# Spreading a softmax over the steps of a matmul loop, and moving its sums to another PSUM bank

## The chip, the cores and the metric

One core of a Trainium2 chip. The metric is device time in microseconds, the median of several executions. All runs quoted were fast, at a granted TensorE clock of 0.995 to 1.000. Single executions of one kernel mostly lie within 1 us of each other; now and then one is 1 to 2.7 us longer.

## The reference, cut to what matters

```python
qn = q / (np.linalg.norm(q, axis=1, keepdims=True) + 1e-06)     # B, N, C = 4, 5824, 256
kn = k / (np.linalg.norm(k, axis=1, keepdims=True) + 1e-06)
s = kn.transpose(0, 2, 1) @ qn / tau                            # 256 x 256 per batch
a = softmax(s)                                                  # over the last axis
x = (v @ a).reshape(B * N, C)
out = ((x @ w1) * (x @ w2)) @ w3 @ w_out                        # 1024 wide inside
```

The softmax is small (256 x 256 per batch). Nearly all the work is the chain of matmuls over 23,296 tokens.

## The kernel before

For each batch the kernel folds the softmax matrix into w1 and w2 ("folds", eight products into `Wf`). Then it runs 11 chunks of 512 tokens and one short chunk of 192 columns. A chunk has eight **steps**. A step makes two products a and b (two matmuls of 512 columns each), evacuates a with ScalarE (`as`), multiplies it with b on VectorE (`abs`), and multiplies an earlier `abs` by the last weights into `out`, two steps behind.

During batch b the kernel also prepares batch b+1: the products G of q and k, their norms, the softmax, the folds. These are items of an agenda. Each has a time on the kernel's own schedule clock, which advances by the estimated TensorE time of what is emitted, and items come out between two steps only.

```python
def k_row():                      # norms of k, four ScalarE operations in a row
    ...
    nc.scalar.activation(out=kr, in_=src, func=AF.Ln)
    nc.scalar.activation(out=kr, in_=kr, func=AF.Exp, scale=0.5)
    nc.scalar.activation(out=kr, in_=kr, func=AF.Ln, bias=eps_t)
    nc.scalar.activation(out=kr, in_=kr, func=AF.Exp, scale=-1.0)
...
def scale(ct):                    # VectorE reads G
    nc.vector.tensor_mul(st["s"][:, ct, :], G_tiles[n][:, ct, :], st["kr"])

def exps():                       # ScalarE
    for ct in range(CT):          # CT = 2
        nc.scalar.activation(out=e[:, ct, :], in_=st["s"][:, ct, :], func=AF.Exp, scale=st["r"][:, ct : ct + 1])

def scaled():
    for ct in range(CT):
        scale(ct)
    exps()
...
# PSUM tiles of 512 fp32: G 1, ab 4 (a, b, folds, sums), out 3
st["sum"] = psum.tile([P, 512], F32, tag="out" if n == 0 else "ab", ...)
...
head = [(0.0, norms), (0.0, k_row), (0.0, q_sums)]      # q_sums ends with r: two small ScalarE operations
return head + [(0.0, scaled), (0.2, sums)] + [(0.43, lambda i=i: fold(i)) for i in range(8)]
...
def run_due(upto=None):           # called between steps
    lim = clock[0] if upto is None else upto
    while agenda and agenda[0][0] <= lim:
        ...
...
ts = [t1 + 1.0] + [t1 + late + t for t in (8.5, 9.0, 11.0, 14.5)] + [t1 + late + 15.5 + 0.9 * i for i in range(8)]
```

## Time and profile before

| | before |
|---|---|
| median | 575.26 us (6 runs, 574.97 to 577.88; the prediction had the first three, 575.4) |
| span of the profiled run | 573.5 us |
| TensorE busy | 559.5 us, 98% |
| idle TensorE around the softmax of batches 1, 2, 3 | 0.60, 1.07, 1.07 us |

A busy share is how much of the span an engine had work in it. TensorE at 98% still leaves 14 us idle: 7.2 in the first 40 us, 4.0 in the last 13.5, and 2.7 around the three softmaxes. I also use one measure that the profile doesn't print: the **stretch** from the first full-width product a of one batch to that of the next, from the starts in the timeline of TensorE, in the one profiled execution of each kernel. Each contains one softmax, it includes idle time that modelled matmul ends hide, and it doesn't see the start of the kernel.

| stretch with the softmax of batch | before |
|---|---|
| 1 (40.53 to 182.70) | 142.17 us |
| 2 (to 316.47) | 133.77 us |
| 3 (to 449.91) | 133.44 us |
| the rest, to the last matmul (569.41) | 119.50 us |

The last has no softmax; it is 119.49 or 119.50 in all twelve profiled kernels, so this measure can tell tenths of a microsecond apart. The lines of the profile before are shown in the prediction.

### The profile page before, as it was taken

What the parts mean: (1) busy time and instruction counts of PE and PEld (TensorE: products, weight loads), DVE (VectorE), ACT (ScalarE), POOL (GpSimd) and SP (SyncE); (2) the same over time, 40 slices, a digit from 0 to 9 for tenths busy, and PEclk for the clock granted to TensorE, in tenths of its full rate; (3) what the DMA queues carried; (4) which work ended last, traced back from release to release, by engine and by line L of the source; (5) the groups of instructions that cost most, each with busy time, mean ns of one, the idle gap of its engine ahead of it and who ended that gap; (6) DMA issues with size and microseconds to landing.
All of it is one profiled execution on the core that took longest, in us unless ns stands there. A gap on an engine that the chain in (4) does not pass through costs nothing.

```text
span 573.5 us, 10096 instructions
## 1 busy us (share of the span) xinstructions
PE 559.5 (98%) x3744; PEld 354.8 (62%) x3750; DVE 377.3 (66%) x612; ACT 337.4 (59%) x624; POOL 82.9 (14%) x164
## 2 busy tenths in 40 slices
PE   8889999999999999999999999999999999999997
PEld 4755576776665666666666666666665666666565
DVE  1047744788877567887776567778876656565564
ACT  0046635777856567776756567767756554454453
POOL 5250020312030111111030012021120000000000
PEclk9999999999999999999999999999999999999999
DMA  8999959769675698495661595675740325221011
GB/s 161 211 194 209 179 99 240 183 153 234 137 174 118 137 191 151 91 192 120 145 147 55 113 203 132 133 142 120 183 110 38 84 73 147 63 62 75 38 70 59
DMA packets 74560, 76.93 MB, mean 134 GB/s; under 512 B 54160, under 2 KB 58256, under 8 KB 74512
## 3 DMA queue, kind: packets, MB, share of 16 engines
q0 software_dynamic: 15504, 39.46, 38.9%
q1 hardware_dynamic: 58784, 36.64, 22.1%
q8 instruction: 29, 0.48, 0.3%
q10 hardware_dynamic: 224, 0.20, 0.1%
q14 instruction: 19, 0.16, 0.1%
HBM read 78.91 MB, written 23.86 MB: 179 GB/s over the span
## 4 chain that ended last, share of the span: by engine, by line
PE 86%; DMA 6%; ACT 4%; DVE 2%; issue 1%; POOL 1%; ACTq 0%; DVEq 0%; POOLq 0%
PE o L470 26%; PE a L429 26%; PE b L429 26%; PE G L188 5%; DMA k<-in_k_dram 5%; PE fold L348 2%; ACT as L435 2%; DVE abs L444 1%; DMA w<-in_moe_w_dram 1%; PE w L587 1%; ACT e L311 0%; POOL k L109 0%; ACT kr L273 0%; POOL q L109 0%; DVE osb L491 0%
## 5 line engine op out<-in xcount | busy, mean ns | idle before, releaser
L444 DVE TENSOR_TENSOR abs<-as,b 128x512 bf16<-128x512 bf16 x336 | 229.9, 686 | 141.0 <-ACT as L435 130.4
L435 ACT CAST as<-a 128x512 bf16<-128x512 f32 (+1 forms) x384 | 215.3, 562 | 179.4 <-DVE abs L444 92.2
L429 PEld LDWEIGHTS <-Wf 128*128 128x128 bf16 x1536 | 149.2, 98 | 102.6 <-issue 2.1
L429 PE MATMUL a<-vT,Wf 128*128 128x512 bf16 x704 | 209.4, 379 | 0.5 <-ACT as L435 0.5
L470 PE MATMUL o<-W_sb,abs 128*128 128x256 bf16 x1376 | 209.6, 273 | 0.1
L429 PE MATMUL b<-vT,Wf 128*128 128x512 bf16 x704 | 209.3, 379 | 0.0
L470 PEld LDWEIGHTS <-abs 128*128 128x128 bf16 x1376 | 134.4, 98 | 81.6 <-DVE abs L446 0.3
L197 DVE TENSOR_TENSOR acc<-acc,sq 128x1024 f32<-128x1024 f32 x66 | 80.4, 1219 | 0.2 <-ACT sq L185 0.2
L188 PE MATMUL G<-k,q 128*128 128x256 bf16 x276 | 49.7, 273 | 0.0
L185 ACT ACTIVATE sq<-q 128x512 f32<-128x512 bf16 x66 | 41.8, 633 | 0.0
L185 ACT ACTIVATE sq<-k 128x512 f32<-128x512 bf16 x66 | 41.6, 630 | 0.0
L417 POOL COPY gate_t<-abs 1x1 bf16<-1x1 bf16 x39 | 13.8, 354 | 168.8 <-DVE abs L444 167.9
L491 DVE COPY osb<-o 128x512 f32<-128x512 f32 x44 | 30.1, 685 | 0.7 <-PE o L470 0.7
L188 PEld LDWEIGHTS <-q 128*128 128x128 bf16 x276 | 27.0, 98 | 3.1
L421 POOL COPY gate_t<-vT 1x1 bf16<-1x1 bf16 x17 | 4.3, 255 | 170.3 <-DMA vT<-v 161.8
L490 ACT COPY osb<-o 128x512 f32<-128x512 f32 x44 | 25.8, 586 | 4.1 <-PE o L470 2.1
L271 ACT ACTIVATE kr<-row 128x256 f32<-128x256 f32 x1 | 0.4, 383 | 31.6 <-PE row L266 31.6
L109 POOL DMA_DIRECT2D q<-in_q_dram x29 | 15.6, 539 | 12.9 <-DMA k<-in_k_dram 5.6
L348 PE MATMUL fold<-w,e 128*128 128x512 bf16 x61 | 16.8, 379 | 0.5 <-DMA w<-in_moe_w_dram 0.2
L355 ACT ACTIVATE Wf<-fold,rs 128x512 bf16<-128x512 f32 x16 | 10.9, 687 | 7.9 <-PE fold L348 6.5
L109 POOL DMA_DIRECT2D k<-in_k_dram x25 | 13.7, 548 | 3.9 <-DMA k<-in_k_dram 1.9
L109 POOL DMA_DIRECT2D v<-in_v_dram x25 | 13.5, 543 | 4.0 <-issue 2.7
(90 smaller groups left out, 227.2 us busy)
## 6 DMA issues: line engine op xcount, KB each, us to landing
out_dram<-osb SPq DMA_DIRECT2D x44, 512.0 KB, 3.0
k<-in_k_dram POOLq DMA_DIRECT2D x19, 512.0 KB, 8.6
v<-in_v_dram POOLq DMA_DIRECT2D x19, 512.0 KB, 5.3
q<-in_q_dram POOLq DMA_DIRECT2D x18, 512.0 KB, 6.5
w_wout<-in_moe_w_dram POOLq DMA_DIRECT2D x1, 2048.0 KB, 23.4
k<-in_k_dram POOLq DMA_DIRECT2D x4, 320.0 KB, 9.8
v<-in_v_dram POOLq DMA_DIRECT2D x4, 320.0 KB, 5.5
q<-in_q_dram POOLq DMA_DIRECT2D x4, 256.0 KB, 11.9
```

What stands on the lines that cost most here:

```text
L109: nc.gpsimd.dma_start(out=pieces[nm, n, pi][:, lo:hi, :], in_=qk_main[nm, n][0][:, pi * PIECE + lo : pi * PIECE + hi, :])
L185: nc.scalar.activation(out=dst[:, :, part, :], in_=src[:, o : o + 2, :], func=AF.Square)
L188: nc.tensor.matmul(G[:, ct, :], lhsT=qt[:, i, ct * P : (ct + 1) * P], rhs=kt[:, i, :], start=(pr == 0 and part == 0 and ct == 0), stop=(pr ...
L197: nc.vector.tensor_add(accs[n], accs[n], sqs[0])
L348: nc.tensor.matmul(st["fold", i], lhsT=st["e"][:, c2, c1 * P : (c1 + 1) * P], rhs=w12[:, c2, w, h * 512 : (h + 1) * 512], start=(c2 == 0), ...
L417: nc.gpsimd.tensor_copy(gate_t, last_ab[0][:1, :1])
L429: nc.tensor.matmul(t[:, :n], lhsT=Wf[b][:, ct, w, j * P : (j + 1) * P], rhs=rhs_of(b, c, ct), start=(ct == 0), stop=(ct == CT - 1),)
L435: nc.scalar.copy(a_sb[:, :n], tiles[0][:, :n])
L444: nc.vector.tensor_mul(ab, a_sb, tiles[1])
L470: nc.tensor.matmul(tl[h][:, o, :], lhsT=lhsT, rhs=W_sb[:, j, :], start=(j == 0 and o == 0), stop=(j == FT - 1 and (small or o == 1)), skip ...
L490: nc.scalar.copy(o[:, 0:2, :], tl[0])
L491: nc.vector.tensor_copy(o[:, 2:4, :], tl[1])
```

## The change

Its intent: the softmax of batches 1 to 3 no longer comes as bursts on ScalarE but as single operations between evacuations, and its sums no longer take one of the four ab buffers but the bank of G, which is idle once the scales have read it.

```diff
-            kr = work.tile([P, C], F32, tag="kr", name=f"kr_{n}", bufs=1)
-            nc.scalar.activation(out=kr, in_=src, func=AF.Ln)
-            ... (three more)
+            st["row"] = src
+            st["kr"] = work.tile([P, C], F32, tag="kr", name=f"kr_{n}", bufs=1)
+            if n == 0:
+                for i in range(4):
+                    k_step(i)
+
+        def k_step(i):
+            kr = st["kr"]
+            nc.scalar.activation(
+                out=kr, in_=kr if i else st["row"], func=(AF.Ln, AF.Exp)[i % 2],
+                scale=(1.0, 0.5, 1.0, -1.0)[i], bias=eps_t if i == 2 else 0.0,
+            )
 ...
-                st["sum"] = psum.tile([P, 512], F32, tag="out" if n == 0 else "ab", name=f"sum_{n}", bufs=3 if n == 0 else 4)
+                st["sum"] = psum.tile([P, 512], F32, tag="out" if n == 0 else "G", name=f"sum_{n}", bufs=3 if n == 0 else 1)
 ...
-        head = [(0.0, norms), (0.0, k_row), (0.0, q_sums)]
-        return head + [(0.0, scaled), (0.2, sums)] + [(0.43, lambda i=i: fold(i)) for i in range(8)]
+        return (
+            [(0.0, 0.0, norms), (0.0, 6.0, k_row)]
+            + [(0.0, 6.0 + 1.3 * i, lambda i=i: k_step(i)) for i in range(4)]
+            + [(0.0, 6.5, q_sums), (0.0, 9.3, lambda: q_norm(st["ss"]))]
+            + [(0.0, 11.3 + 1.3 * ct, lambda ct=ct: scale(ct)) for ct in range(CT)]
+            + [(0.0, 12.0 + 1.3 * ct, lambda ct=ct: exps(ct)) for ct in range(CT)]
+            + [(0.2, 15.5, sums)]
+            + [(0.43, 16.5 + 0.85 * i, lambda i=i: fold(i)) for i in range(8)]
+        )
 ...
-            t0, t1 = 57.0, 116.0
+            t0, t1 = 57.0, 115.5
 ...
-        late = 2.5 if b == 0 else 0.0
-        ts = [t1 + 1.0] + [t1 + late + t for t in (8.5, 9.0, 11.0, 14.5)] + ...
+        for i, (cst, t, fn) in enumerate(soft):
+            at(t1 + 1.0 + t + (2.0 if b == 0 and i > 0 else 0.0), cst, fn)
```

(`exps` takes the half as an argument, and batch 0 calls the same operations in the old order. By its new times the change also moves the scales, the sums and the folds up to two clock units later.)

More of the change, by code (lines that the diff above doesn't have):

```diff
@@ L250, in scaled_first @@
             scale(1)
-            exps()
+            exps(0)
+            exps(1)
         def norms():
@@ L269, in k_row @@
                 src = st["tot"][:, 1, :]
-            kr = work.tile([P, C], F32, tag="kr", name=f"kr_{n}", bufs=1)
-            nc.scalar.activation(out=kr, in_=src, func=AF.Ln)
-            nc.scalar.activation(out=kr, in_=kr, func=AF.Exp, scale=0.5)
-            nc.scalar.activation(out=kr, in_=kr, func=AF.Ln, bias=eps_t)
-            nc.scalar.activation(out=kr, in_=kr, func=AF.Exp, scale=-1.0)
-            st["kr"] = kr
+            st["row"] = src
[9 more added lines that the diff above has]
+            )
         def diagonal(src):
@@ L290, in q_sums @@
         def q_sums():
-            q_norm(diagonal(st["tot"][:, 0, :].rearrange("p (c t) -> p c t", t=P)))
+            st["ss"] = diagonal(st["tot"][:, 0, :].rearrange("p (c t) -> p c t", t=P))
         def q_norm(src):
@@ L306, in scale, with exps @@
             nc.vector.tensor_mul(st["s"][:, ct, :], G_tiles[n][:, ct, :], st["kr"])
-        def exps():
-            e = work.tile([P, CT, C], BF16, tag="e", name=f"e_{n}", bufs=2)
-            for ct in range(CT):
-                nc.scalar.activation(
-                    out=e[:, ct, :], in_=st["s"][:, ct, :], func=AF.Exp, scale=st["r"][:, ct : ct + 1]
-                )
-            st["e"] = e
-        def scaled():
-            for ct in range(CT):
-                scale(ct)
-            exps()
+        def exps(ct):
+            if ct == 0:
+                st["e"] = work.tile([P, CT, C], BF16, tag="e", name=f"e_{n}", bufs=2)
+            nc.scalar.activation(
+                out=st["e"][:, ct, :], in_=st["s"][:, ct, :], func=AF.Exp, scale=st["r"][:, ct : ct + 1]
+            )
         def sum_mm(c2):
             if c2 == 0:
-                st["sum"] = psum.tile([P, 512], F32, tag="out" if n == 0 else "ab", name=f"sum_{n}", bufs=3 if n == 0 else 4)
+                st["sum"] = psum.tile([P, 512], F32, tag="out" if n == 0 else "G", name=f"sum_{n}", bufs=3 if n == 0 else 1)
                 Wf[n] = wf_pool.tile([P, CT, 2, F], BF16, tag="Wf", name=f"Wf_{n}")
@@ L377, in soft_units @@
             return [k_first, k_row, q_first, scaled_first, first_folds] + [lambda i=i: fold(i) for i in range(6, 8)]
-        head = [(0.0, norms), (0.0, k_row), (0.0, q_sums)]
-        return head + [(0.0, scaled), (0.2, sums)] + [(0.43, lambda i=i: fold(i)) for i in range(8)]
+        return (
[6 more added lines that the diff above has]
+            + [(0.43, 16.5 + 0.85 * i, lambda i=i: fold(i)) for i in range(8)]
+        )
     clock = [0.0]
@@ L648, in make_agenda @@
         soft = soft_units(n)
-        late = 2.5 if b == 0 else 0.0
-        ts = [t1 + 1.0] + [t1 + late + t for t in (8.5, 9.0, 11.0, 14.5)] + [t1 + late + 15.5 + 0.9 * i for i in range(8)]
-        for t, (cst, fn) in zip(ts, soft):
-            at(t, cst, fn)
+        for i, (cst, t, fn) in enumerate(soft):
+            at(t1 + 1.0 + t + (2.0 if b == 0 and i > 0 else 0.0), cst, fn)
         agenda.sort()
```

## The prediction

> **What bounds the kernel now.** I read the page first, then the waits of TensorE, then busy time by stretch, then the timeline around a softmax.
>
> ```profile
> PE 559.5 (98%) x3744; PEld 354.8 (62%) x3750; DVE 377.3 (66%) x612; ACT 337.4 (59%) x624; POOL 82.9 (14%) x164
> ...
> PE 86%; DMA 6%; ACT 4%; DVE 2%; issue 1%; POOL 1%; ACTq 0%; DVEq 0%; POOLq 0%
> ```
>
> TensorE is the bound: busy 98%, and 86% of the chain that ended last. Busy could hide slowness, so I checked the pace. One step of the main loop is four matmuls of 512 columns (a and b) and four of 256 (out), and it starts every 1.30 us (a at 419.68, 420.98, 422.28), which is full rate at a granted clock of 0.999. So only idle time of TensorE can be won, and where it idles is told by its waits.
>
> ```profile
> PE sqq L221 <- DMA q<-in_q_dram: 3.9, 3, 2.1
> PE sum L327 <- ACT as L435: 1.6, 2, 0.8
> PE sum L327 <- ACT e L311: 1.2, 1, 1.2
> ...
> PE a L429 <- ACT as L435: 0.7, 3, 0.2
> ```
>
> The DMA wait and the 1.2 us for e belong to batch 0 at the start, which the change leaves alone. What remains is the softmax of batches 1 to 3. By stretch (length, busy PE, PEld, DVE, ACT, POOL, clock, DMA):
>
> ```profile
> 172.00:184.00 12.00, 11.40 (x82) 6.87 (x81) 8.38 (x28) 7.94 (x18) 0.66 (x2) 1.00 0.60 132
> 184.00:292.00 108.00, 108.00 (x696) 67.85 (x694) 81.28 (x110) 73.56 (x132) 18.11 (x36) 1.00 0.69 147
> ...
> 300.00:304.00 4.00, 2.93 (x22) 1.67 (x20) 2.66 (x7) 2.42 (x5) 0.00 (x0) 1.00 0.61 185
> ...
> 434.00:438.00 4.00, 2.93 (x22) 1.67 (x20) 2.66 (x7) 2.42 (x5) 0.00 (x0) 1.00 0.35 135
> ```
>
> TensorE idles 0.60, 1.07 and 1.07 us in the three softmaxes and nowhere in the 108 us between two of them. **The most that a perfect softmax saves is about 2.7 us**, 0.5%, plus small gaps that matmul ends hide. The timeline of batch 3 shows the cause:
>
> ```profile
> 431.33 0.42 ACT L274 ACTIVATE kr<-kr 128x256 f32<-128x256 f32 x1
> 431.66 0.19 ACT L295 ACTIVATE r<-ss 128x2 f32<-128x2 f32 x1
> 431.88 0.20 ACT L296 ACTIVATE r<-r 128x2 f32<-128x2 f32 x1
> 431.99 1.05 ACT L435 CAST as<-a 128x512 bf16<-128x512 f32 x2
> ...
> 434.39 0.75 DVE L306 TENSOR_TENSOR s<-G,kr 128x256 f32<-128x256 f32 x2
> ...
> 434.84 0.91 ACT L311 ACTIVATE e<-s,r 128x256 bf16<-128x256 f32 x2 [1.31 <-DVE s L306]
> ...
> 435.65 1.05 ACT L435 CAST as<-a 128x512 bf16<-128x512 f32 x2
> ...
> 436.26 0.24 PE L327 MATMUL sum<-ones_b,e 128*128 128x1 bf16 x4 [0.82 <-ACT as L435]
> ...
> 436.75 0.59 PE L429 MATMUL a<-vT,Wf 128*128 128x512 bf16 x2 [0.25 <-ACT as L435]
> ```
>
> Undisturbed, evacuations (as) start every 1.30 us: 428.11, 429.41, then due at 430.71, 432.01, 433.31, 434.61. The first burst of six small ScalarE operations makes one start at 431.99, 1.28 us late, and TensorE does not stop. The second burst, two exps behind a wait for s, makes one start at 435.65, 2.34 us late, and TensorE stops for 0.82 us: the sums need a buffer of the ab group, and all four are full. **So about 1.3 us of lateness is absorbed.** By arithmetic: an evacuation starts 0.63 us after its product and takes 0.58, and its buffer is wanted 2.60 after the product, so 1.39 is the slack.
>
> **What the Trainium skill says.** "TensorE: Matmul & The Clock Gate", "Wait — 56ns, not 53.3ns?": start to start is N/2.4 GHz plus about 2.5 ns; 4x215.8+4x109.2 = 1300 ns, and the trace agrees (1.30). The same page, "Architectural detail: the array is 16× 32×32, not 1× 128×128": ScalarE and VectorE are strict FIFO. The trace agrees: the evacuation due at 433.31 stands behind the exps, though its product began at 432.68. "ScalarE: Activation LUTs", "What ACT_TABLE_LOAD costs": an ACTIVATE takes 186 ns + 0.833 per element, 93 more for each pointer operand, and neighbours overlap by about 93. For 256 elements: 399, and 492 with the pointer; the trace has 417, 508 (bias) and 500 (exp), with as to as 0.47 apart. "PSUM — Partial Sum Buffer", "Specifications (TRN2)": eight banks of 2 KiB. The kernel has G 1, ab 4, out 3: none is free for the sums but G's own, idle once s is read.
>
> **The change, part by part.** It removes and adds no instruction; batch 0 runs as before.
>
> (1) The four kr operations and the two of r are spread. That burst cost nothing, so this wins nothing itself.
>
> (2) The sums go to G's bank. They no longer wait for an evacuation, only for e, and the ring of four is not lent out for a product.
>
> (3) scale and exp are split per half. The aim is a scale in one step and its exp in the next. Whether that happens is set by the kernel's own schedule clock: a step charges 1.300 and items come out only between steps. I worked the boundaries out. In batch 1 (softmax of 2) they are at 12.065+1.3m (two first steps 1.945, scores 46x0.22), in batch 2 (softmax of 3) at 12.283+1.3m, in batch 0 (softmax of 1) at 18.567+1.3K. For batch 2 the scales at 116.3 and 117.6 come out at m=81 and 82, and the exps at 117.0 and 118.3 also at 81 and 82. The same for batch 3. **So each exp still stands directly behind its scale**, only one pair per step. For batch 1 they do separate: scales at K=86, 87, exps at 87, 88.
>
> Cost of a pair in one step, from starts in the trace: evacuation to product on VectorE 0.62 (160.92 to 161.54), to s 0.60 (433.79 to 434.39), to exp 0.45 (434.39 to 434.84), exp to next evacuation 0.40 (half of 434.84 to 435.65): 2.07 instead of 1.30, 0.77 late. Two in a row: 1.54 late, for batch 2 some 0.15 more, because its fourth kr operation comes in one step with an output copy. Against 1.39: TensorE stops 0.15 to 0.3, partly while it runs the sums. Batch 3 has another snag: its first fold comes out in the same step as the sums, and its evacuation waits on ScalarE for the reciprocal, about a step; I put 0.3 there, and 0.1 for four folds in a row in batch 2.
>
> Sum: batch 2, 1.07-0.15-0.1 = 0.8; batch 3, 1.07-0.15-0.3 = 0.6; batch 1: the first product of its short chunk starts at 173.67 instead of the due 173.29, and its outputs at 174.40 instead of 173.62, so 0.78 if all goes. There the folds also come a step or two later, into short steps that lose about 0.8 us between them (17,920 columns take 7.6 us at the pace above, the stretch 173.67 to 182.70 took 9.03; part of that is the stop): fewer steps share with a fold, perhaps 0.1. Together 2.3. All of it is on the path, since TensorE is the path from 62 us on. 575.4-2.3 = **573.1, put at 573.2**.
>
> **Rivals.** (A) The exps behind their scales stop TensorE as much as before, only at another place: for it, the coinciding steps in batches 2 and 3 and the VectorE queue, where s stands behind a 0.69 us product; against it, the halves are a step apart and 1.3 us was absorbed before. Then only batch 1 gains: 574.5 to 575. (B) All stalls vanish, the short chunk included: 575.4-2.7-0.6 = 572.1. (C) An earlier kr waits for the all-reduce on GpSimd (3.23 us): for batch 1 it ends at 165.73 and the first kr would stand behind the output copy at about 165.9; for batch 3 it ends at 427.44 and kr is due at 427.3. A wait of 0.2 inside the slack: nothing. (D) More buffers for the ring start transfers earlier: no, loads are gated by products.
>
> **Range and chances.** B gives the lower end, A the upper, and runs of the same kernel lie from 575.35 to 577.88, most within 0.1. 8 in 10: 572.2 to 575.2. A gain of 2% would need 11.5 us, four times all the idle time there is; a loss of 2% would need a new stall of 4 us in each softmax. Chances: faster 0.01, same 0.98, slower 0.01.
>
> **What would show it.** Right: TensorE's waits no longer list the sums behind an evacuation; kr operations stand singly between evacuations; in batches 2 and 3 each exp still shows a wait for s of some 0.6 to 1.2 us; idle in those softmaxes falls from 1.07 to below 0.5. Wrong: idle stays near 1 us there (A), the folds' evacuations show waits of over 1 us for rs, or the sums wait for e by more than 0.3. It would be far off only if the rotation of the ab buffers brought a stall into every step, which nothing in the diff does.

## The result, and the profile after

The kernel after takes **573.24 us** (median of 6, 572.82 to 573.53) against 575.26. The ratio of the two is 0.9959, 95% interval 0.9942 to 0.9976. A ratio here is the mean time of one kernel's fast runs over that of the other's of the same rounds, so not quite the ratio of the medians. The prediction said 573.2, range 572.2 to 575.2.

The page after, busy line and chain that ended last:

```profile
PE 559.4 (98%) x3750; PEld 354.5 (62%) x3750; DVE 377.4 (66%) x612; ACT 337.7 (59%) x624; POOL 83.3 (15%) x164
...
PE 92%; DMA 5%; DVE 1%; ACT 1%; POOL 1%; issue 0%; ACTq 0%; POOLq 0%
```

The work is the same, to 0.1 us of TensorE. ScalarE's part of the chain fell from 4% to 1%: the end is less often set by an evacuation. TensorE's waits after (total, times, longest):

```profile
PE sqq L221 <- DMA q<-in_q_dram: 3.9, 3, 1.9
PE sum L328 <- ACT e L318: 1.2, 1, 1.2
...
PE a L438 <- ACT as L444: 0.3, 1, 0.3
```

The 1.6 us of sums behind evacuations are gone, and of 0.7 us of products behind evacuations 0.3 is left. By stretch (length, busy PE, PEld, DVE, ACT, POOL, clock, DMA):

```profile
172.00:184.00 12.00, 11.86 (x87) 7.21 (x86) 8.85 (x27) 7.81 (x19) 0.53 (x1) 1.00 0.61 132
...
300.00:304.00 4.00, 3.89 (x28) 2.41 (x27) 1.91 (x5) 2.35 (x5) 0.00 (x0) 1.00 0.46 153
...
434.00:438.00 4.00, 4.00 (x28) 2.26 (x27) 2.51 (x6) 1.85 (x4) 0.00 (x0) 1.00 0.15 54
438.00:450.00 12.00, 11.59 (x83) 7.28 (x81) 8.44 (x25) 7.60 (x17) 0.00 (x0) 1.00 0.11 45
```

Idle TensorE is now 0.14, 0.11 and 0.00 us where it was 0.60, 1.07 and 1.07. But the last row idles 0.41 us, where the kernel before has this:

```profile
438.00:450.00 12.00, 11.95 (x88) 8.11 (x88) 8.97 (x23) 7.29 (x17) 0.00 (x0) 1.00 0.11 42
```

So in batch 3 something is given back later. The stretches say how much:

| stretch with the softmax of batch | before | after | gain |
|---|---|---|---|
| 1 | 142.17 | 141.43 | 0.74 |
| 2 | 133.77 | 132.76 | 1.01 |
| 3 | 133.44 | 133.21 | 0.23 |

Their sum is 1.98; the profiled run after entered batch 0's first product 0.16 later (40.69), which leaves 1.83, and the profiled spans differ by just that (573.5 to 571.7). What ScalarE does around the softmax of batch 3 after the change, from its timeline:

```profile
430.42 0.59 ACT L444 CAST as<-a 128x512 bf16<-128x512 f32 x1
431.07 0.59 ACT L499 COPY osb<-o 128x512 f32<-128x512 f32 x1
431.72 0.59 ACT L444 CAST as<-a 128x512 bf16<-128x512 f32 x1
433.40 0.51 ACT L318 ACTIVATE e<-s,r 128x256 bf16<-128x256 f32 x1 [1.09 <-DVE s L313]
433.81 0.57 ACT L444 CAST as<-a 128x512 bf16<-128x512 f32 x1
435.47 0.51 ACT L318 ACTIVATE e<-s,r 128x256 bf16<-128x256 f32 x1 [1.09 <-DVE s L313]
435.88 1.06 ACT L444 CAST as<-a 128x512 bf16<-128x512 f32 x2
438.13 0.69 ACT L356 ACTIVATE Wf<-fold,rs 128x512 bf16<-128x512 f32 x1 [1.19 <-DVE rs L335]
```

Each exp waits 1.09 us for its scale (bracketed: how long the engine stood idle before, and for whom): the two are in one step, not apart, as the prediction had worked out. From one evacuation to the next it is 2.09 and 2.07 us (predicted 2.07), so the second is 1.56 late (predicted 1.54). Then the first fold's evacuation holds ScalarE 1.19 us for the reciprocal of the sums. TensorE pays behind that:

```profile
438.29 1.65 PE L349 MATMUL fold<-w,e 128*128 128x512 bf16 x6
440.07 0.59 PE L438 MATMUL a<-vT,Wf 128*128 128x512 bf16 x2
...
441.37 1.46 PE L349 MATMUL fold<-w,e 128*128 128x512 bf16 x6
442.66 0.33 PE L438 MATMUL a<-vTt,Wf 128*128 128x192 bf16 x2
...
446.60 0.33 PE L438 MATMUL a<-vTt,Wf 128*128 128x192 bf16 x2 [0.27 <-ACT as L444]
```

Three folds take 1.78 us to the next product (438.29 to 440.07), the next three 1.29: 0.49 lost, and 0.27 more in the short chunk.

### The profile page after: what moved, and what is told of

Same layout as the page of the kernel before. It is cut to its first block, busy times and chain, and to the rows that moved or that the text cites. A ratio compares the mean times of both kernels' runs of the same rounds, so it can differ in the third digit from the quotient of the medians.

```text
span 571.7 us, 10102 instructions
## 1 busy us (share of the span) xinstructions
PE 559.4 (98%) x3750; PEld 354.5 (62%) x3750; DVE 377.4 (66%) x612; ACT 337.7 (59%) x624; POOL 83.3 (15%) x164
## 4 chain that ended last, share of the span: by engine, by line
PE 92%; DMA 5%; DVE 1%; ACT 1%; POOL 1%; issue 0%; ACTq 0%; POOLq 0%
PE o L479 28%; PE a L438 27%; PE b L438 27%; PE G L188 5%; DMA k<-in_k_dram 5%; PE fold L349 2%; PE w L596 1%; ACT as L444 0%; ACT kr L279 0%; POOL k L109 0%; POOL q L109 0%; DVE abs L453 0%; PE sqk L221 0%; DVE vT L136 0%; DVE abs L455 0%
```

## The experiments

**Theory.** What counts is how late an evacuation starts against its due time, which is 0.63 us after the start of its product. Up to 1.39 us the four buffers hide it; what lies above, TensorE stands still. Lateness adds up over everything on ScalarE and VectorE since they were last on time. **Rivals**: the exps in a burst are the cause, as the change's intent has it; the bank of the sums is; or, taken from the prediction, the burst of kr costs nothing and spreading it wins nothing.

All kernels below gave correct results. The kernel before was run beside each group: medians 575.11, 575.00 and 575.11 us. The last three columns are the stretches with the softmax of batches 1, 2 and 3.

| run | what it is | median us | 1 | 2 | 3 |
|---|---|---|---|---|---|
| before | | 575.26 | 142.17 | 133.77 | 133.44 |
| after | the change | 573.24 | 141.43 | 132.76 | 133.21 |
| u1_k_burst | after, kr and r in a burst | 573.92 | 141.43 | 133.06 | 133.54 |
| u2_exp_burst | after, scales and exps in a burst | 572.53 | 141.66 | 132.49 | 132.36 |
| u3_sum_ab | after, sums in ab | 573.53 | 141.42 | 133.19 | 133.21 |
| a1_k_alone | before, kr and r spread | 573.56 | 141.76 | 133.22 | 132.89 |
| a2_sum_alone | before, sums in G's bank | 574.53 | 142.18 | 133.34 | 133.01 |
| d1_two_more_exps | u2, each exp twice | 575.66 | 144.37 (1.5 of it a load) | 133.57 | 133.59 |
| f1_folds_later | after, folds later | 572.58 | 141.09 | 132.99 | 132.72 |
| a3_exp_step_later | after, each exp a step later | 572.23 | 141.42 | 132.46 | 132.37 |
| b1_exps_next_step | after, both scales, then both exps | 571.98 | 141.42 | 132.46 | 132.35 |
| g1_exps_and_folds_later | a3 and f1 | 571.91 | 142.47 (1.2 of it a load) | 132.70 | 132.27 |

### One part undone

**The spread of kr.**

```diff
-            [(0.0, 0.0, norms), (0.0, 6.0, k_row)]
-            + [(0.0, 6.0 + 1.3 * i, lambda i=i: k_step(i)) for i in range(4)]
-            + [(0.0, 6.5, q_sums), (0.0, 9.3, lambda: q_norm(st["ss"]))]
+            [(0.0, 0.0, norms), (0.0, 7.5, k_row)]
+            + [(0.0, 7.5, lambda i=i: k_step(i)) for i in range(4)]
+            + [(0.0, 7.7, q_sums), (0.0, 7.7, lambda: q_norm(st["ss"]))]
```

> The change with one part undone: the four kr operations and the two of r are again one burst, where the kernel before had it; the split of the exps and the bank of the sums stay. Theory: lateness of the evacuations adds up, and TensorE stops only when an evacuation starts more than about 1.39 us late. The burst itself is absorbed (1.28 late), but it leaves VectorE behind, so the two coinciding scale-exp pairs start from a later point: the evacuation after the second exp some 2.0 late in batches 2 and 3 instead of 1.54. I expect 0.4 us more of TensorE idle in each of the two, none in batch 1: 573.24+0.8 = 574.0. Rival, step 1 of the prediction taken literally (the spread wins nothing itself): 573.2, as the change.

Measured: 573.92 us, 0.68 more than after, and 0.30 and 0.33 more in the stretches of batches 2 and 3, none in batch 1. ScalarE in batch 3:

```profile
431.73 0.61 ACT L444 CAST as<-a 128x512 bf16<-128x512 f32 x1
433.76 0.51 ACT L318 ACTIVATE e<-s,r 128x256 bf16<-128x256 f32 x1 [1.42 <-DVE s L313]
434.18 0.57 ACT L444 CAST as<-a 128x512 bf16<-128x512 f32 x1
435.83 0.51 ACT L318 ACTIVATE e<-s,r 128x256 bf16<-128x256 f32 x1 [1.09 <-DVE s L313]
436.25 1.05 ACT L444 CAST as<-a 128x512 bf16<-128x512 f32 x2
```

The product of the evacuation at 436.25 began at 433.61, so it was due 0.63 later, at 434.24: 2.01 late, as expected. The burst does cost, though TensorE doesn't stop behind it: it leaves VectorE behind. The first scale starts 2.30 us after the start of its step (433.31 after 431.01), in the change 1.85 (432.94 after 431.09), and these 0.45 us are what the evacuation is later than there (2.01 against 1.56). (The burst stands three steps before the scales here and two in the kernel before, since the change moved the scales too.)

**The split of the exps.**

```diff
-            + [(0.0, 11.3 + 1.3 * ct, lambda ct=ct: scale(ct)) for ct in range(CT)]
-            + [(0.0, 12.0 + 1.3 * ct, lambda ct=ct: exps(ct)) for ct in range(CT)]
+            + [(0.0, 11.3, lambda ct=ct: scale(ct)) for ct in range(CT)]
+            + [(0.0, 11.3, lambda ct=ct: exps(ct)) for ct in range(CT)]
```

> The change with one part undone: both scales and both exps come out in one step again, as in the kernel before; kr stays spread and the sums stay in the bank of the products. Theory of lateness: one burst costs 0.62+0.60+0.45+0.40+0.40 = 2.47 us from one evacuation to the next instead of 1.30, so 1.17 late, once, which is below 1.39: no stop, while the split pairs of the change are 1.54 late. So the same as the change within 0.1 us: 573.2, TensorE idle in the softmax of batches 2 and 3 not above the change's. Rival, the aim of the change (the exps are what has to be set apart): the stop of the kernel before comes back at the products, some 0.5 to 0.8 us in each of the three: 574.7 to 575.2.

Measured: 572.53 us, **0.7 us less than the whole change**. The idle did not come back. ScalarE in batch 3:

```profile
431.33 0.58 ACT L444 CAST as<-a 128x512 bf16<-128x512 f32 x1
433.00 0.91 ACT L318 ACTIVATE e<-s,r 128x256 bf16<-128x256 f32 x2 [1.09 <-DVE s L313]
433.82 1.05 ACT L444 CAST as<-a 128x512 bf16<-128x512 f32 x2
```

One wait of 1.09 us for both exps; the next evacuation, due at 432.63, is 1.19 late (expected 1.17), below 1.39. Split, the wait is paid twice. The theory's number, the same as the change within 0.1, was missed, and the rival's too: batch 3 gained 0.85. Its first fold still waits for the reciprocal (1.08 us here), but with less lateness this no longer stops TensorE. In batch 1, where the change's exps are apart, the burst loses 0.23.

**The bank of the sums.**

```diff
-  st["sum"] = psum.tile([P, 512], F32, tag="out" if n == 0 else "G", name=f"sum_{n}", bufs=3 if n == 0 else 1)
+  st["sum"] = psum.tile([P, 512], F32, tag="out" if n == 0 else "ab", name=f"sum_{n}", bufs=3 if n == 0 else 4)
```

> The change with one part undone: the sums are again in one of the four ab buffers. Theory: in batches 2 and 3 the sums then wait for the evacuation behind the second exp (0.2 to 0.3 us), and the next product for the one after it: 0.3 to 0.45 us more each. Batch 1 has no late evacuation there: nothing. 573.24+0.7 = 573.9. Rival, once the exps are apart a buffer of ab is always free and the bank no longer matters: 573.2.

Measured: 573.53 us, 0.29 more than after, all of it in batch 2 (0.43). In batch 3 TensorE does wait at the sums and the first fold (0.25 us), but the stretch is unchanged: the later stop of batch 3 absorbs it. So half of the expectation held.

### One part alone

**kr and r spread** (the edit to `k_row` as in the change; in the agenda):

```diff
-        ts = [t1 + 1.0] + [t1 + late + t for t in (8.5, 9.0, 11.0, 14.5)] + ...
+        ts = [t1 + 1.0] + [t1 + late + t for t in (6.0, 6.0, 7.3, 8.6, 9.9, 6.5, 9.0, 11.0, 14.5)] + ...
```

> The kernel before with one part of the change alone: kr and r spread over four steps; scales and exps in one burst at the old step, sums in ab. Theory of lateness: without the burst of six, VectorE isn't behind when the scales come, so the evacuation behind the exps is 1.17 late in batch 1 (no stop) and about 1.8 instead of 2.34 in batches 2 and 3, where the output copy of a chunk stands just before: idle 0.78 less in batch 1, about 0.5 less in each of the others: 575.26-1.8 = 573.5. Rival, step 1 of the prediction taken literally (the burst of kr cost nothing, so spreading it wins nothing): 575.2.

Measured: 573.56 us, 1.55 less than before. Of the change's 2.0 us, spreading kr alone brings three quarters. The spread kr also begins 2.5 clock units earlier than the burst did; a burst that only comes earlier was not tried. ScalarE in batch 3:

```profile
431.18 0.58 ACT L443 CAST as<-a 128x512 bf16<-128x512 f32 x1 [0.40 <-PE a L437]
431.83 0.58 ACT L498 COPY osb<-o 128x512 f32<-128x512 f32 x1
433.45 0.91 ACT L318 ACTIVATE e<-s,r 128x256 bf16<-128x256 f32 x2 [1.04 <-DVE s L313]
434.27 1.05 ACT L443 CAST as<-a 128x512 bf16<-128x512 f32 x2
```

The evacuation due at 432.48 is 1.79 late, where the kernel before was 2.34 late. Batches 2 and 3 gained 0.55 each, as expected; batch 1 only 0.41 instead of 0.78: its evacuation is 1.19 late and the next product is on time, but the first short step still takes 1.01 us, where it takes 0.77 with the exps apart (a3).

**The sums in G's bank** (the edit to `st["sum"]` alone):

> The kernel before with one part of the change alone: the sums in the bank of the products. Theory: in batches 2 and 3 the sums no longer wait for the late evacuation but only for the second exp (about 0.35 us instead of 0.82), and the next product takes the buffer that the sums had: 0.5 us less idle in each of the two; nothing in batch 1, whose sums come when the short products have freed buffers. 575.15-1.0 = 574.1. Rival: the product waits for the same late evacuation instead, and only the wait's name changes: 575.1.

Measured: 574.53 us, 0.47 less than before; the stretches of batches 2 and 3 fell by 0.43 each. The medians show about half of that, within their scatter (the interval of the ratio is 0.9979 to 1.0004), so the time alone would not have settled this one. TensorE's waits show the exchange:

```profile
PE sum L327 <- ACT e L311: 1.6, 3, 1.2
...
PE a L429 <- ACT as L435: 0.8, 3, 0.3
```

The sums now wait 0.2 us each for the exp instead of 0.8 for a buffer.

### The slack, measured

Each exp of batches 1 to 3 written twice, in the version with one burst (u2):

```diff
-            nc.scalar.activation(out=st["e"][:, ct, :], ...)
+            for _ in range(1 if n == 0 else 2):
+                nc.scalar.activation(out=st["e"][:, ct, :], ...)
```

> The version with one burst of exps (572.53 us) with each exp of batches 1 to 3 done twice, the same values written again: two more ScalarE operations of 0.40 in that burst, so the evacuation behind it is 2.0 us late instead of 1.19. Theory of slack: TensorE stops for what lies above 1.39, 0.6 us in each of the three batches: 572.53+1.8 = 574.3. Rivals: if ScalarE had no slack, 0.8 each: 574.9 or more; if its lateness weren't what stops TensorE: 572.5.

Measured: 575.66 us, 3.1 more than u2 rather than 1.8. In batch 2, ScalarE, then TensorE:

```profile
301.63 0.58 ACT L445 CAST as<-a 128x512 bf16<-128x512 f32 x1
303.30 1.99 ACT L319 ACTIVATE e<-s,r 128x256 bf16<-128x256 f32 x4 [1.09 <-DVE s L313]
305.19 1.05 ACT L445 CAST as<-a 128x512 bf16<-128x512 f32 x2
```

```profile
304.31 0.60 PE L480 MATMUL o<-W_sb,abs 128*128 128x256 bf16 x4
305.80 0.59 PE L439 MATMUL a<-vT,Wf 128*128 128x512 bf16 x2 [0.90 <-ACT as L445]
```

The evacuation belongs to the product that began at 302.14, so it was due at 302.77 and is 2.42 late, not 2.0: the first of the two is itself 0.16 late, and the four exps took 0.47 each, where I had put 0.40 (two of them write the same tile again, which may be why; it was not tested alone). The product due at 304.74 started at 305.80, a stop of 1.06, against 2.42-1.39 = 1.03. In batches 1 and 3 the lateness is 2.27 and the stop 0.92, against 0.88. So **the slack is 1.36 us**, within 0.03 of the arithmetic. My miss was the size of the dose, not the slack. These stops are nearly all that batch 2 lost (1.08); batch 3 lost 1.23, 0.28 of it at one step of its short chunk. Batch 1's stretch of this profile also holds a wait of 1.5 us for a load of k, which is not the exps' doing; that execution took 577.34, the other four 575.3 to 575.9.

### Mending what the change left

**The folds half a unit later**, so that batch 3's first fold doesn't share a step with the sums:

```diff
-            + [(0.43, 16.5 + 0.85 * i, lambda i=i: fold(i)) for i in range(8)]
+            + [(0.43, 17.0 + 0.85 * i, lambda i=i: fold(i)) for i in range(8)]
```

> The change with the folds half a clock unit later, so that in batch 3 the first fold comes a step after the sums, as in batch 2, and its evacuation no longer waits on ScalarE for the reciprocal. This tests the fold step of the prediction. Theory (lateness adds up: two late exps plus this wait): batch 3's stretch falls from 133.21 by 0.4 to 0.6; batch 2's stays within 0.15 of 132.76; batch 1's within 0.2 of 141.43, since one more fold comes after its short products. 572.8. Rival (the exps alone cost batch 3): 573.2.

Measured: 572.58 us. Batch 3 gains 0.49, as expected; batch 1 gains 0.34, more than I allowed for; batch 2 loses 0.23, more than I allowed for. One fold more now lies among the short products of batch 2; that this is the cause is argued, not shown.

**Each exp a step later**, so that it is a step behind its scale in every batch:

```diff
-            + [(0.0, 12.0 + 1.3 * ct, lambda ct=ct: exps(ct)) for ct in range(CT)]
+            + [(0.0, 13.0 + 1.3 * ct, lambda ct=ct: exps(ct)) for ct in range(CT)]
```

> The change with each exp moved one step later in batches 2 and 3, so that scale and exp are really apart there (in batch 1 they already are). Theory: no evacuation is then late by more than 0.2 us, ScalarE shows no wait for s in batches 1 to 3, and the stretches of batches 2 and 3 (first product of a batch to first product of the next) fall from 132.76 and 133.21 to those of the run with one burst of exps, 132.49 and 132.36, or just below: 573.24-1.1 = 572.1 to 572.4. Rival: what batch 3 loses is the fold that shares a step with the sums, and separate exps don't mend it: 573.0.

Measured: 572.23 us, 1.0 less than the change. ScalarE in batch 3:

```profile
431.40 0.59 ACT L444 CAST as<-a 128x512 bf16<-128x512 f32 x1
432.70 0.59 ACT L444 CAST as<-a 128x512 bf16<-128x512 f32 x1 [0.71 <-DVE abs L453]
433.18 0.51 ACT L318 ACTIVATE e<-s,r 128x256 bf16<-128x256 f32 x1
434.00 0.59 ACT L444 CAST as<-a 128x512 bf16<-128x512 f32 x1 [0.31 <-PE a L438]
434.48 0.51 ACT L318 ACTIVATE e<-s,r 128x256 bf16<-128x256 f32 x1
```

No wait for s, evacuations every 1.30 us. The stretches of batches 2 and 3 fall to 132.46 and 132.37, with the folds where they were. This is what the change was meant to be; it missed it by a phase of the schedule clock.

**Both exps in the step after both scales:**

```diff
-            + [(0.0, 11.3 + 1.3 * ct, lambda ct=ct: scale(ct)) for ct in range(CT)]
-            + [(0.0, 12.0 + 1.3 * ct, lambda ct=ct: exps(ct)) for ct in range(CT)]
+            + [(0.0, 11.3, lambda ct=ct: scale(ct)) for ct in range(CT)]
+            + [(0.0, 13.0, lambda ct=ct: exps(ct)) for ct in range(CT)]
```

> The change with both scales in one step and both exps together in the next, in each of batches 1 to 3. It tells apart two readings of why the split costs in batches 2 and 3: theory, an exp behind its own scale makes ScalarE wait about 1.1 us and that wait, not the number of exps in a step, is what makes evacuations late. Then here the evacuation behind the two exps is at most 0.2 us late although they stand together, and the stretches are 132.5 and 132.4 as with the exps one step later (572.23 us): 572.2. Rival, two exps in one step are too many: 0.4 to 0.8 us more in each batch, 573.4 or more.

Measured: 571.98 us and the stretches of a3 within 0.02. ScalarE in batch 3:

```profile
431.01 0.58 ACT L444 CAST as<-a 128x512 bf16<-128x512 f32 x1
432.31 0.58 ACT L444 CAST as<-a 128x512 bf16<-128x512 f32 x1 [0.71 <-DVE abs L453]
432.79 0.91 ACT L318 ACTIVATE e<-s,r 128x256 bf16<-128x256 f32 x2
433.61 0.58 ACT L444 CAST as<-a 128x512 bf16<-128x512 f32 x1
```

So the exps need not be single. What makes the evacuations late is the wait of an exp for a scale in the same step. One such wait fits into the slack: u2, with one per batch, is within 0.03 of these stretches in batches 2 and 3, and only in batch 1 0.24 longer. Two in a row, or one behind other lateness, do not fit.

**a3 with the folds later:**

> The version with each exp one step later (572.23 us), with the folds half a unit later too: the best that these parts give together. If lateness was all that the fold's wait for the reciprocal could hurt through, batch 3 stays at 132.37 within 0.1 and batch 2 at 132.46 within 0.25, and only batch 1 gains the 0.3 us that its later folds gave before (141.43 to 141.09): 571.9. If the fold's wait costs by itself, batch 3 falls by 0.3 to 0.5 more: 571.5.

Measured: 571.91 us. Batch 3 gains 0.10 only: with the evacuations on time, the fold's wait costs nearly nothing by itself. Batch 2 loses 0.24 again. Batch 1's stretch holds a wait of 1.2 us for a load of k in the profiled execution (573.15 us; the other four 571.7 to 571.9), which leaves about 141.3, so hardly a gain. This and b1 are the fastest; their medians are 0.07 apart, which is no difference. Both beat the kernel before (ratios 0.9944 and 0.9947) and the change.

## Why the prediction was right or wrong

The time was right, 573.24 for 573.2. That it came this close is partly luck: a gain of 2.2 from 575.4 was predicted and 2.02 from 575.26 measured, and by batch the misses are -0.16, +0.21 and -0.37. By its own steps:

- **"The most that a perfect softmax saves is about 2.7 us, plus small gaps."** Right: the best version gained 3.2 us.
- **"Each exp still stands directly behind its scale" in batches 2 and 3, apart in batch 1.** Right: waits of 1.09 us for s, four of them, none in batch 1. The pair cost 2.07 to 2.09 us, predicted 2.07. Rival B, all stalls gone, was therefore out, and a3 shows that the coincidence was what kept it out: with it mended, 572.23, close to B's 572.1. In batch 2 the second evacuation was 1.71 late (the working: 1.54+0.15), and from the sums to the next product it took 0.35 us, 0.25 more than in u2, within the 0.15 to 0.3 predicted.
- **"About 1.3 us of lateness is absorbed", slack 1.39.** Right; d1 measures 1.36.
- **Part (1), "That burst cost nothing, so this wins nothing itself."** Wrong. It was read from TensorE's idle alone. Spread alone (a1) it brings 1.55 of the 2.0 us, and undone (u1) it costs 0.68. The lateness of 2.34 behind the exps was not theirs alone: a burst of exps by itself makes 1.19 (u2) or, behind an output copy, 1.79 (a1); the rest was VectorE still behind from the first burst. The sum came out right since I counted the whole stop as removed, whichever part removes it.
- **Part (2), the bank.** Right, 0.43 each in batches 2 and 3 alone; on top of the other parts only batch 2 keeps it.
- **Part (3), the split.** I took it as a gain that falls short. It gains 0.23 in batch 1, but in batches 2 and 3 it is a loss (0.27 and 0.85): u2, without it, is 0.7 us faster.
- **The sum by batch:** 0.8+0.1, 0.8 and 0.6 predicted; 0.74, 1.01 and 0.23 measured. The total, 2.3, was put at 2.2 and is 2.0. The mis-sized term is batch 3's fold, 0.3 (0.45 with the late exps); batch 3 lost 0.84 of its 1.07. The mechanism was there (a wait of 1.19 us for rs), but it adds to the late exps: taking away either one brings most back (f1 0.49, u2 0.85).
- **"The folds' evacuations show waits of over 1 us for rs"** was listed as a sign of being wrong, though the working itself counted on it. It came true in batch 3 and cost what the bullet above says.
- **Two figures on the way are off**, and nothing hung on them. The short steps of batch 1 lose 1.0 us by its own numbers, not 0.8 (9.03-7.6 = 1.43, of which 0.40 is the stop). And 11.5 us is four times the idle time of the softmaxes, not "all the idle time there is", which is 14 us.
- **Rival A** (the exps stop TensorE as before) nearly came true in batch 3, together with the fold, and not in batch 2. **Rival C** (kr waits for the all-reduce) did not happen: no such wait in the list of waits. **Rival D** (loads that come earlier and collide): the profiled run of the change has no wait for a load after batch 0's first product, as before. Two profiles of other variants have one of 1.2 to 1.5 us for k in batch 0; what brings it in some executions stays open.

## What to carry to other kernels

Measure a disturbance by how late the engine comes back to its beat, not by whether the bound engine stopped just then: a burst that is absorbed uses up the slack of the next one. Rather than split a burst up, put each operation a full step behind the one that it waits for; two independent ones in a row cost little (b1: the next evacuation was at most 0.1 us late). When a schedule emits items at step boundaries only, work out which boundary each one falls on, since a distance of half a step can round to none.

## What the Trainium skill lacked or had wrong

- "ScalarE: Activation LUTs", "What ACT_TABLE_LOAD costs", says that neighbouring ACTIVATEs overlap by about 93 ns. That held for independent ones (evacuations of 584 ns start 0.47 us apart, exps of 500 ns 0.40). For dependent ones it doesn't: kr operations of 417 ns start 0.45 apart, one reading what the other wrote, and exps that write one tile again averaged 0.47.
- No page tells what a chain of dependent operations on ScalarE and VectorE costs in a loop. Start to start in the profile before: evacuation to product 0.62 us, product to scale 0.60, scale to exp 0.45, exp to the next evacuation 0.40, so 2.07 for a pair where a step has 1.30. Nearly all of it is the operations themselves: the product starts 0.04 us after the end of the evacuation, and in the change the exp 0.04 after the end of the scale.
- "PSUM — Partial Sum Buffer", "Summary: rules for kernel authors", says to evacuate promptly, but no page says how late is too late. With four buffers shared by two products per step, it was 1.36 us of lateness at 1.30 us per step.
